# Two engines empty one PSUM result, a bank each, and the rounds of the second product are spread anew over a half block

## The chip, the cores and the metric

One core of one Trainium2 chip. The time is device time in microseconds (us) of one launch; a quoted time is the median of several executions. All executions of this study were of the same (fast) state, but those of one kernel still scatter by 2 to 4 us; the section on the start tells where much of that comes from. Where a few us matter I use the ratio of the mean times in the same rounds on the same chip, with its 95% interval.

## The reference

A causal convolution of 7 taps over time (softmaxed weights, one set per head of 24 channels), then a two-layer network with ELU, on 32768 tokens of 192 channels:

```python
# attention part: out[b,s,h,:] = sum_k softmax(weight)[h,k] * x_padded[b, s+k, h, :]
h = x @ w_in                                   # 192 -> 2048
g = np.where(h > 0.0, h, np.exp(np.minimum(h, 0.0)) - 1.0)
return (g @ w_out).astype(np.float32)          # 2048 -> 192
```

## The kernel before

The tokens go in 32 blocks of 1024; a block has 16 **pairs**, one for each 128 of the 2048 hidden channels. A pair is two products of 512 tokens, in one of three two-bank PSUM buffers H. ScalarE takes exp of it, GpSimd clamps it to at most 1, VectorE takes the maximum with h (I call its two instructions the pair's **clips**) and so frees the buffer. In the cuts, `W(s, n)` waits until semaphore `s` has counted to `n`:

```python
    # ScalarE, pair n
    W(s_h, n + 1)
    W(s_tt, 2 * (n - NE) + 2)
    for u in range(2):
        a.activation(E[:, n % NE, u, :], H[:, k, GS * u : GS * (u + 1)], ACT.Exp).then_inc(s_exp)
    # VectorE, pair n
    for n in range(NP):
        ...
        for u in range(2):
            W(s_clp, 2 * n + u + 1)
            v.scalar_tensor_tensor(out=gT[:, s % NG3, q, u, :], in0=E[:, n % NE, u, :], scalar=1.0,
                in1=H[:, slot_of_pair[n] % 3, GS * u : GS * (u + 1)],
                op0=ALU.subtract, op1=ALU.max).then_inc(s_tt)
```

The second product adds up in the last two banks, `ops`. It comes in **rounds** of two matmuls of 64x192, 64 rounds to a **half** of a block (256 + 256 tokens), placed in the gaps behind the pairs by a list of sizes. One conv (the convolution over time, for a later block) also stands in each half and takes a turn of the H buffers. When a half is done, ScalarE copies both banks at once:

```python
LAG = -3
GAPS = ((10,), (10,), (6,), (6,), (10,), (5, 6), (11,))     # rounds behind each pair of a half
EARLY_CONV = {3: (1, 0), 6: (1, 1), 9: (2, 0)}              # the first three convs, by pair
X_LATE = (17, 3, 2)                                         # an extra load of x, ahead of pair 17's clamp
...
    # ScalarE, end of a half
    W(s_swap, mm2_done[key])
    ...
    a.activation(osb[:, b, :, :, :].rearrange("p g k d -> p g (k d)"),
                 ops[:, :, 0 : 2 * D], ACT.Copy).then_inc(s_oev)
    # TensorE, first round of the next half
    W(s_oev, place[key])
```

## Time and profile before

| | before |
|---|---|
| time | 747.96 us (747.39 to 748.05, 3 executions) |
| steady block of 16 pairs | 22.54 us (27 blocks) |
| pair 10 / pair 16 begin | 28.2 / 35.9 us |
| VectorE / ScalarE / GpSimd busy | 85 / 87 / 89% |

A "steady block" is the time from the start of a pair to the start of the 16th pair after it, the mean from block 3 to block 29.

### The profile page before, as it was taken

The numbers are of one execution on the slowest core, as the hardware profiler recorded it, in microseconds if no ns is written. First come the engines' busy times: TensorE is split into PE (matmuls) and PEld (weight loads), VectorE is DVE, ScalarE is ACT, GpSimd is POOL, SyncE is SP. The second block draws the span as 40 slices with busy tenths as digits, with TensorE's granted clock in tenths as the row PEclk, the third lists the DMA queues.
The fourth block names the chain that finished last, engine by engine and source line by source line (L and its number), as shares of the span: only waits on it lengthen the run. The fifth ranks groups of instructions, "written<-read, shape, count | busy, mean of one in ns | idle before, by whom it ended". The sixth has DMA issues, their size and how long they took to land.

```text
span 746.5 us, 28038 instructions
## 1 busy us (share of the span) xinstructions
PE 731.6 (98%) x11866; PEld 505.4 (68%) x11866; DVE 638.0 (85%) x1042; ACT 646.8 (87%) x1224; POOL 664.5 (89%) x1108
## 2 busy tenths in 40 slices
PE   6899999999999999999999999999999999999997
PEld 3466667666766676666766766766766766766666
DVE  5789889889889888898898898898898898888894
ACT  4888988988988988888989989989989989889883
POOL 8799999999899999899999899999999899898893
PEclk9999999999999999999999999999999999999999
DMA  9544435535435535345535345635345444244212
GB/s 168 93 76 91 62 70 93 94 61 92 63 68 94 93 60 95 57 74 95 82 71 94 46 84 94 77 77 70 64 91 94 67 87 81 53 89 81 46 44 66
DMA packets 132881, 58.93 MB, mean 79 GB/s; under 512 B 98068, under 2 KB 132372, under 8 KB 132756
## 3 DMA queue, kind: packets, MB, share of 16 engines
q0 software_dynamic: 44160, 17.28, 22.9%
q1 hardware_dynamic: 88308, 39.37, 21.9%
q8 instruction: 93, 1.52, 0.9%
q10 hardware_dynamic: 288, 0.49, 0.2%
q14 instruction: 32, 0.26, 0.1%
HBM read 35.61 MB, written 25.17 MB: 81 GB/s over the span
## 4 chain that ended last, share of the span: by engine, by line
PE 93%; DVE 2%; POOL 2%; DMA 1%; ACT 1%; issue 0%
PE H L735 45%; PE ops L770 44%; PE H L703 3%; DVE gT L579 2%; DMA xg<-in_x_dram 1%; ACT E L515 1%; POOL E L414 1%; PE H L770 1%; POOL w_in L369 1%; ACT csb L485 0%; POOL xg L364 0%; PE ops L703 0%; ACT osb L474 0%; PE ops L615 0%; POOL sel L384 0%
## 5 line engine op out<-in xcount | busy, mean ns | idle before, releaser
L579 DVE SCALAR_TENSOR_TENSOR gT<-E,H 128x512 f16<-128x512 f32 x1024 | 632.5, 681 | 90.9 <-POOL E L414 84.4
L414 POOL TENSOR_SCALAR E<-E 128x512 f32<-128x512 f32 x1024 | 603.9, 615 | 69.5 <-ACT E L515 62.1
L515 ACT ACTIVATE E<-H 128x512 f32<-128x512 f32 x1024 | 546.2, 608 | 73.5 <-PE H L735 64.8
L770 PE MATMUL ops<-w_out,gT 64*128 64x192 f16 x8064 | 426.4, 243 | 0.3
L770 PEld LDWEIGHTS ops<-w_out,gT 64*128 64x128 f16 x8064 | 346.9, 94 | 110.5 <-ACT osb L474 11.4
L735 PE MATMUL H<-att,w_in 64*128 64x512 bf16 x3072 | 409.2, 378 | 2.9 <-DVE gT L579 1.7
L735 PEld LDWEIGHTS H<-att,w_in 64*128 64x128 bf16 x3072 | 130.9, 94 | 111.7 <-DVE gT L579 12.8
L485 ACT ACTIVATE csb<-H 128x480 bf16<-128x480 f32 x118 | 60.9, 568 | 7.4 <-PE H L703 0.4
L474 ACT ACTIVATE osb<-ops 128x768 f32<-128x768 f32 x63 | 52.0, 826 | 6.2 <-PE ops L770 6.2
L364 POOL DMA_DIRECT2D xg<-in_x_dram x62 | 55.7, 899 | 0.1
L703 PE MATMUL H<-xg,Tm 64*128 64x240 bf16 x472 | 44.0, 263 | 0.1
L703 PEld LDWEIGHTS H<-xg,Tm 64*128 64x128 bf16 x472 | 21.2, 94 | 0.8 <-DVE gT L579 0.3
L485 ACT ACTIVATE csb<-ops 128x480 bf16<-128x480 f32 x6 | 3.5, 588 | 3.2 <-PE ops L703 3.2
L770 PE MATMUL H<-w_out,gT 64*128 64x192 f16 x128 | 5.9, 243 | 0.0
L703 PE MATMUL ops<-xg,Tm 64*128 64x240 bf16 x24 | 2.7, 306 | 3.3 <-DMA xg<-in_x_dram 3.1
L590 DVE COPY osb<-H 128x192 f32<-128x192 f32 x1 | 0.4, 358 | 6.3 <-PE H L770 6.3
L770 PEld LDWEIGHTS H<-w_out,gT 64*128 64x128 f16 x128 | 5.3, 94 | 0.0
L369 POOL DMA_DIRECT2D w_in<-in_moe_w_in_dram x7 | 4.6, 663 | 0.3 <-DMA wh<-in_weight_dram 0.3
L610 PE MATMUL ops<-zw 128*128 128x512 bf16 x9 | 3.6, 577 | 1.2 <-DVE zw L527 1.2
L615 PE MATMUL ops<-zw 64*128 64x512 bf16 x12 | 2.4, 381 | 2.3 <-ACT csb L485 2.3
L703 PEld LDWEIGHTS ops<-xg,Tm 64*128 64x128 bf16 x24 | 0.9, 97 | 5.2 <-issue 3.5
L615 PEld LDWEIGHTS ops<-zw 64*128 64x128 bf16 x12 | 0.6, 93 | 4.2 <-ACT csb L485 3.9
(49 smaller groups left out, 26.3 us busy)
## 6 DMA issues: line engine op xcount, KB each, us to landing
out_dram<-osb SPq DMA_DIRECT2D x126, 192.0 KB, 4.1
xg<-in_x_dram POOLq DMA_DIRECT2D x61, 240.0 KB, 5.6
w_out<-in_moe_w_out_dram POOLq DMA_DIRECT2D x1, 768.0 KB, 16.1
att<-csb SPq DMA_TRANSPOSE x31, 6.4
w_in<-in_moe_w_in_dram POOLq DMA_DIRECT2D x2, 240.0 KB, 9.0
xf<-in_x_dram ACTq DMA_DIRECT2D x1, 384.0 KB, 3.2
xf<-in_x_dram SPq DMA_DIRECT2D x1, 384.0 KB, 3.6
w_in<-in_moe_w_in_dram POOLq DMA_DIRECT2D x2, 144.0 KB, 4.2
```

The source lines that it names most:

```text
L364: g.dma_start(xg[:, b, v0 : v0 + whole, :], src).then_inc(s_x[b][part - 1], 16)
L369: g.dma_start(w_in[HP * r : HP * (r + 1), :, c0:c1], moe_w_in.rearrange("(p j) f -> p j f", j=3)[:, :, c0:c1],).then_inc(s_w[k], 16)
L414: g.tensor_scalar(out=E[:, n % NE, u, :], in0=E[:, n % NE, u, :], scalar1=1.0, scalar2=0.0, op0=ALU.min, op1=ALU.max,).then_inc(s_clp)
L474: a.activation(osb[:, b, :, :, :].rearrange("p g k d -> p g (k d)"), ops[:, :, 0 : 2 * D], ACT.Copy,).then_inc(s_oev)
L485: return a.activation(csb[:, s % 2, :].rearrange("p (j v h i) -> p h j v i", j=3, v=2 * WPG, h=HEADS)[:, h0 : h0 + HB], conv_bank(m)[:, b, ...
L515: a.activation(E[:, n % NE, u, :], H[:, k, GS * u : GS * (u + 1)], ACT.Exp).then_inc(s_exp)
L579: v.scalar_tensor_tensor(out=gT[:, s % NG3, q, u, :], in0=E[:, n % NE, u, :], scalar=1.0, in1=H[:, slot_of_pair[n] % 3, GS * u : GS * (u + ...
L610: pe.matmul(ops[:, 0, :], zw[:, 0:P], zw[:], start=True, stop=True)
L615: pe.matmul(ops[:, r, :], zw[HP * r : HP * (r + 1), 0:P], zw[HP * r : HP * (r + 1), :], start=True, stop=True, tile_position=(HP * r, 0),)
L703: ins = pe.matmul(to[:, b, n1 * hh : n1 * (hh + 1)], Tm[HP * rt : HP * (rt + 1), h, :], xg[HP * rt : HP * (rt + 1), s % NXB, :, :].rearran ...
L735: ins = pe.matmul(H[:, k % 3, GS * r : GS * (r + 1)], w_in[HP * r : HP * (r + 1), j, FC * q : FC * (q + 1)], att[HP * r : HP * (r + 1), s ...
L770: ins = pe.matmul(acc[:, g, d0 : d0 + D], gT[HP * rt : HP * (rt + 1), t % NG3, q, g, t0 : t0 + P], w_out[HP * rt : HP * (rt + 1), q, :], s ...
```

## The change

Its intent: the two banks leave on two engines at once, so the evacuation is over sooner and ScalarE is relieved; the rounds are spread so that two light gaps follow the evacuation; and the first convs stand later, so that they don't wait for x.

```diff
-LAG = -3
-GAPS = ((10,), (10,), (6,), (6,), (10,), (5, 6), (11,))
+LAG = -5
+GAPS = ((), (1,), (16,), (7,), (7,), (7,), (6,), (7, 3, 10))
-EARLY_CONV = {3: (1, 0), 6: (1, 1), 9: (2, 0)}
+EARLY_CONV = {6: (1, 0), 8: (1, 1), 10: (2, 0)}
...
+            load_x(2, 2)
             g.dma_start(w_out ...)
-            load_x(2, 2)
...
-                a.activation(osb[:, b, ...], ops[:, :, 0 : 2 * D], ACT.Copy).then_inc(s_oev)
+                out_ready(W, key)
+                a.activation(*out_pieces(key, 0), ACT.Copy).then_inc(s_oev)
...  # VectorE
-            for n in range(NP):
+            for item in order:
+                if item[0] == "o":
+                    for key in item[2]:
+                        out_ready(W, key)
+                        v.tensor_copy(*out_pieces(key, 1)).then_inc(s_od)
+                elif item[0] == "h":
                     ...
...  # TensorE
                                 W(s_oev, place[key])
+                                W(s_od, place[key])
```

The end of the half now lies in the conv's own gap: 7 rounds, half a conv, 3 rounds, the other half, 10 rounds. VectorE's copy stands, in its program, behind the clips of that pair.

More of the change, by code (lines that the diff above doesn't have):

```diff
@@ L24 @@
 BN = HB * CPH * 2 * WPG
-GAP_SPLIT = 4
 TAP = 6
@@ L84, in bass_lightweight_conv__then__act_elu_kernel, with conv_at @@
     order = []
-    def conv_at(s, g, gap=None):
+    def conv_at(s, g, between=None):
         m = 2 * s + g - 2
@@ L90, in conv_at @@
         order.append(("c", m, 0))
-        between = []
-        if gap:
-            between, gap[:] = gap[:GAP_SPLIT], gap[GAP_SPLIT:]
         if between:
@@ L139, in bass_lightweight_conv__then__act_elu_kernel @@
         gaps = list(rounds_at.get(n, ()))
-        if len(gaps) == 2:
-            order.append(("o", gaps.pop(0)))
-        if n in EARLY_CONV:
-            conv_at(*EARLY_CONV[n])
-        if s:
-            for at, ahead, g in CONV_AT:
-                if at == i and s + ahead < NS:
-                    conv_at(s + ahead, g, gaps[0] if gaps else None)
-        if gaps and gaps[0]:
-            order.append(("o", gaps[0]))
+        convs = [EARLY_CONV[n]] if n in EARLY_CONV else []
+        convs += [
+            (s + ahead, g)
+            for at, ahead, g in CONV_AT
+            if at == i and s + ahead < NS and 2 * (s + ahead) + g - 2 >= FREE_CONV
+        ]
+        if convs and len(gaps) == 3:
+            order.append(("o", gaps[0]))
+            conv_at(*convs[0], gaps[1])
+            order.append(("o", gaps[2]))
+            continue
+        for conv in convs:
+            conv_at(*conv)
+        for gap in gaps:
+            order.append(("o", gap))
     last_slot = [take_slot(None) for _ in range(2)]
@@ L326, in out_group, with out_ready, out_pieces @@
             eng.dma_start(dst, osb[:, b, g, :, :]).then_inc(s_out[b], 16)
+        def out_ready(W, key):
+            t, half, kb = key
+            n_half = 2 * t + half
+            W(s_swap, mm2_done[key])
+            W(s_out[n_half % 2], 32 * (n_half // 2))
+        def out_pieces(key, g):
+            t, half, kb = key
+            b = (2 * t + half) % 2
+            if (t, half) == (last, 1):
+                return osb[:, b, g, kb, :], H[:, last_slot[kb] % 3, GS * g : GS * g + D]
+            return (
+                osb[:, b, g, :, :].rearrange("p k d -> p (k d)"),
+                ops[:, g, 0 : 2 * D],
+            )
         def turn_att(eng, s):
@@ L454, in evac @@
             def evac(key):
-                t, half, kb = key
-                n_half = 2 * t + half
-                W(s_swap, mm2_done[key])
-                b = n_half % 2
-                W(s_out[b], 32 * (n_half // 2))
-                if (t, half) == (last, 1):
-                    if kb == 0:
-                        a.activation(
-                            osb[:, b, :, 0, :],
-                            H[:, last_slot[0] % 3, :].rearrange("p (g t) -> p g t", g=2)[:, :, 0:D],
-                            ACT.Copy,
-                        ).then_inc(s_oev)
-                    else:
-                        a.activation(
-                            osb[:, b, 0, 1, :], H[:, last_slot[1] % 3, 0:D], ACT.Copy
-                        ).then_inc(s_oev)
-                        W(s_od, 1)
-                        out_group(a, t, half, 1, 1)
-                    return
-                a.activation(
-                    osb[:, b, :, :, :].rearrange("p g k d -> p g (k d)"),
-                    ops[:, :, 0 : 2 * D],
-                    ACT.Copy,
-                ).then_inc(s_oev)
+                out_ready(W, key)
+                a.activation(*out_pieces(key, 0), ACT.Copy).then_inc(s_oev)
+                if key == (last, 1, 1):
+                    W(s_od, place[key] + 1)
+                    out_group(a, last, 1, 1, 1)
             late = []
@@ L572, in _vector @@
             v.tensor_copy(Tm[:], Tr[:, :, ::-1]).then_inc(s_tm)
-            for n in range(NP):
-                s, q = divmod(n, NQ)
-                if s >= NG3:
-                    W(s_swap, mm2_done[s - NG3, 1, 0])
-                for u in range(2):
-                    W(s_clp, 2 * n + u + 1)
-                    v.scalar_tensor_tensor(
-                        out=gT[:, s % NG3, q, u, :],
-                        in0=E[:, n % NE, u, :],
-                        scalar=1.0,
-                        in1=H[:, slot_of_pair[n] % 3, GS * u : GS * (u + 1)],
-                        op0=ALU.subtract,
-                        op1=ALU.max,
-                    ).then_inc(s_tt)
-            b = (2 * NS - 1) % 2
-            W(s_swap, mm2_done[last, 1, 1])
-            W(s_out[b], 32 * (NS - 1))
-            v.tensor_copy(
-                osb[:, b, 1, 1, :], H[:, last_slot[1] % 3, GS : GS + D]
-            ).then_inc(s_od)
+            for item in order:
[4 more added lines that the diff above has]
+                elif item[0] == "h":
+                    n = item[1]
+                    s, q = divmod(n, NQ)
+                    if s >= NG3:
+                        W(s_swap, mm2_done[s - NG3, 1, 0])
+                    for u in range(2):
+                        W(s_clp, 2 * n + u + 1)
+                        v.scalar_tensor_tensor(
+                            out=gT[:, s % NG3, q, u, :],
+                            in0=E[:, n % NE, u, :],
+                            scalar=1.0,
+                            in1=H[:, slot_of_pair[n] % 3, GS * u : GS * (u + 1)],
+                            op0=ALU.subtract,
+                            op1=ALU.max,
+                        ).then_inc(s_tt)
         @block.tensor
@@ L814, in _sync @@
                         t, half, kb = key
-                        W(s_oev, place[key] + 1)
-                        if (t, half) != (last, 1):
-                            for g in range(2):
+                        for g in range(2):
+                            W((s_oev, s_od)[g], place[key] + 1)
+                            if (t, half) != (last, 1):
                                 out_group(sy, t, half, g)
-                        elif kb == 0:
-                            for g in range(2):
-                                out_group(sy, t, half, g, 0)
-                        else:
-                            out_group(sy, t, half, 0, 1)
+                            elif (g, kb) != (1, 1):
+                                out_group(sy, t, half, g, kb)
             for b in range(2):
```

## The prediction

> **What bounds the kernel now.** I read the page first, then the list of waits, then windows over single stretches, then the timeline of TensorE over one half block. The page gives TensorE 98% of the span, and the chain that ended last is almost all TensorE:
>
> ```profile
> PE 731.6 (98%) x11866; PEld 505.4 (68%) x11866; DVE 638.0 (85%) x1042; ACT 646.8 (87%) x1224; POOL 664.5 (89%) x1108
> ...
> L579 DVE SCALAR_TENSOR_TENSOR gT<-E,H 128x512 f16<-128x512 f32 x1024 | 632.5, 681 | 90.9 <-POOL E L414 84.4
> L414 POOL TENSOR_SCALAR E<-E 128x512 f32<-128x512 f32 x1024 | 603.9, 615 | 69.5 <-ACT E L515 62.1
> L515 ACT ACTIVATE E<-H 128x512 f32<-128x512 f32 x1024 | 546.2, 608 | 73.5 <-PE H L735 64.8
> ...
> L474 ACT ACTIVATE osb<-ops 128x768 f32<-128x768 f32 x63 | 52.0, 826 | 6.2 <-PE ops L770 6.2
> ```
>
> The reader should see three helpers at 85 to 89% behind a nearly full TensorE. Each of the 512 pairs (two 512-wide products into one of three H buffers) passes through ScalarE (exp), GpSimd (clamp) and VectorE (max), and only VectorE's second instruction frees the buffer. The finished output is read by ScalarE once a half, 63 times 826 ns.
>
> "98%" overstates how full TensorE is, because the span of a matmul includes its pipeline: six H matmuls show 0.82 us, but the next work starts 0.65 us after them. So I compare starts with starts. In the timeline of TensorE (start, duration):
>
> ```profile
> 308.13 0.83 PE L735 MATMUL H<-att,w_in 64*128 64x512 bf16 x6
> 308.78 1.01 PE L770 MATMUL ops<-w_out,gT 64*128 64x192 f16 x20
> 309.61 0.83 PE L735 MATMUL H<-att,w_in 64*128 64x512 bf16 x6
> 310.25 0.59 PE L770 MATMUL ops<-w_out,gT 64*128 64x192 f16 x10
> 310.96 0.38 PE L703 MATMUL H<-xg,Tm 64*128 64x240 bf16 x4
> ```
>
> A pair takes 0.65 us and a round (two matmuls side by side) 0.0825 us (0.83 for ten). Five rounds from 310.25 should end at 310.66, yet the conv starts at 310.96: 0.3 us of waiting for a buffer. From the starts of the pairs I took all steady periods: 22.50 or 22.57 us for a block of 16 pairs, so **11.26 us a half** (8 pairs, 64 rounds, one conv). The pure stream is 8 x 0.65 + 64 x 0.0825 + 0.46 for the two conv pieces = 10.94 us. So about 0.3 us a half is stalled, 62 halves x 0.3 = 19 us in all: that is the most that the steady part can give, 2.5% of 748.
>
> Who stalls it, from the list of waits (total us, times, longest):
>
> ```profile
> PEld H L735 <- DVE gT L579: 12.8, 42, 1.4
> PEld ops L770 <- ACT osb L474: 11.4, 62, 0.2
> ...
> PEld ops L615 <- ACT csb L485: 3.9, 3, 1.3
> ...
> PE ops L703 <- DMA xg<-in_x_dram: 3.1, 1, 3.1
> ```
>
> The first row is the H buffer, the second the evacuation. The second is a weight load's wait, 0.18 us each time, and TensorE itself lost none of it: after the 11 rounds come two pairs (1.30 us) without rounds, and the ten rounds after them start on time (313.72 to 315.02 is two pairs exactly). The evacuation is already hidden.
>
> **What the Trainium skill says.** "TensorE: Matmul & The Clock Gate", section "Back-to-back issue gap", gives N/2.4 + 2.5 ns between warm matmuls: 216 ns at 512 and 82.5 ns at 192. The trace agrees: 0.65 us for three side-by-side steps of 512, 0.083 for a round. "PSUM — Partial Sum Buffer", section "Specifications (TRN2)", says that ScalarE and VectorE can read PSUM in parallel at full bandwidth where they are on different banks; the trace has it once, in the very last copy: both started at 742.8 us on a bank each of one result, and took 331 (ScalarE) and 358 ns (VectorE), with no sign of one slowing the other. "VectorE: DVE Perf Modes", section "Why PSUM operands drop a tier", says that fp32 from PSUM runs at the 1x mode: that copy of 128x192 took 358 ns, and VectorE's casts out of PSUM of 256 and 512 columns 425 and 692, so 1.04 ns a column, and 384 columns should take 358 + 192 x 1.04 = 558 ns (estimate).
>
> **The change, part by part.**
>
> 1. Split evacuation. ScalarE: 826 becomes about 484 ns (the row of its 128x384 copy), 63 x 0.34 = 21 us less busy. VectorE: 63 x 0.56 = 35 us more, 638 to some 670 us (90%). The bank pair is free after about 0.6 us instead of 0.9. Since that wait cost TensorE nothing, the direct value is about zero. VectorE does its copy just after the clips of the conv step's pair, where it waits for GpSimd anyway: the next pair begins 2.8 us after that one, VectorE has a gap of about 1.6 us there, and 0.56 fits.
>
> 2. Spread of the rounds. What sets the stalls is how soon a buffer returns. Undisturbed, a pair's second clip ends 3.5 us after the pair begins (3.48 to 3.60 in the steady rows), and TensorE goes on 0.05 later: 3.55. Three buffers rotate, the conv taking a turn. So a pair must not come within 3.55 us of the third place before it, nor faster than VectorE's 1.20 us a pair for long. New half: conv step 0.65 + 7 x 0.0825 + 0.26 + 3 x 0.0825 + 0.25 + 10 x 0.0825 = 2.81; then 0.65 (no rounds), 0.73 (1), 1.97 (16), three of 1.23 (7), 1.15 (6): 11.0 us. Against the rule: the second pair after the conv step would begin 2.81 + 0.65 = 3.46 after the pair whose buffer it takes, a stall of 0.09; the fourth 0.65 + 0.09 + 0.73 + 1.97 = 3.44 after its own, a stall of 0.11; all others are 3.6 or later. Sum 11.2. The same walk over the old half, with VectorE's and GpSimd's queues in it, gives 11.22 where 11.26 is measured, so it is right to about 0.05. **Steady gain 0.02 to 0.06 us a half, near 2 us in 60 halves.** The pile-up moves from the pairs after the long empty stretch to the conv step; it does not go.
>
> 3. Start. Before, the first conv stands behind pair 3 and waits 3.1 us for x, after which the clock is halved:
>
> ```profile
> 18.00:21.40 3.40, 3.00 (x18) 1.17 (x20) 0.00 (x0) 1.09 (x3) 0.00 (x0) 0.51 1.59 193
> ```
>
> (the 0.51 is PEclk.) With the convs behind pairs 6, 8, 10 pairs 4 to 6 run in that time, paced by VectorE. But pair 10 needs the last part of w_in, which is copied within SBUF; that copy is issued at 20.1 us with 6.3 us to landing, so 26.4, and before pair 10 began at 28.2. New: pair 10 at 26.4, its conv, pairs 11 and 12, the first round held to about 30.3 by the conv's second evacuation, pair 13 at 30.4, pair 16 at about 34.9 against 35.9 before, with 5 rounds more done (0.4 us). **Gain 1.5 us**, not the 3 + 2.3 us of the removed waits.
>
> 4. Block 1. It took 23.3 us instead of 22.5, because a load issued on GpSimd (0.9 us) stood before pair 17's clamp and pair 19 waited for that buffer. The two start 0.65 + 6 x 0.0825 + 2.81 = 3.96 us apart in the new order and about 3.5 in the old, so some 0.3 to 0.4 us less is lost.
>
> 5. Tail. Both end in the same rounds and the same two single-bank copies; the last two halves without a conv may wait for the split evacuation, a few tenths. Zero net.
>
> Sum: 2 + 1.5 + 0.3 = 3.8 us; 748.0 - 3.8 = **744.2 us**.
>
> **Rivals.** (a) The stalls do go: the 3.5 us is a little shorter when queues are emptier, the two borderline gaps (3.46 and 3.44) fit, and a half takes 11.0: 60 x 0.25 = 15 us, plus the start, 731. For it: both misses are only about 0.1 us, and the split takes 0.34 us from ScalarE next to those pairs. Against: 3.48 is the minimum that I found, and ScalarE is not what frees the buffer. (b) VectorE becomes the bound: the 0.56 copy pushes the clips behind it, each half loses up to 0.3, some 760 us. For it: at 90% VectorE would be the busiest helper, and it takes its work in order, so a copy waiting for TensorE blocks clips. Against: the gap of 1.6 us. (c) The start gives nothing: an idle of about 3 us before pair 10 halves the clock in turn, as it did before, 746. For it: it is nearly as long as the old wait; against: the skill's first page above, section "What's actually happening", ties the halving to a window of about 3.4 us of idleness, and the idle may be split by window edges. The trace had 3.05 us idle and then 3.4 us at half clock.
>
> **Range and chances.** The steady part is 60 times a difference of -0.05 to +0.1 us, so -3 to +6 us; start and block 1 give 0 to 3. Range 738 to 749. Faster by over 2% (under 733) needs rival (a) almost whole: 0.07. Slower by over 2% (over 763) needs (b) at its worst: 0.03. Within 2%: 0.90.
>
> **What would show it.** Right: ScalarE rows 128x384 near 484 ns and VectorE COPY 128x384 near 560, TensorE's pair starts 11.2 us a half apart with the two small stalls behind the second and fourth pair after the conv step, no wait for xg at the first conv but a wait of some 3 us for w_in before pair 10, pair 16 at about 35. Wrong: halves of 11.0 (rival a) or over 11.3 with VectorE's copies as releaser of ops or H (rival b); a half-clock stretch near 27 us (rival c).

## The result, and the profile after

The change took 743.4 us (742.09 to 745.38, 4 executions); ratio 0.9943, interval 0.9915 to 0.9972. The kernel before took 747.87 us in the same rounds (4 executions). By the ratio the change is 4.3 us faster, and the predicted time was 744.2. A ratio is the mean time of one kernel's fast runs over that of the other's of the same rounds, so not quite the ratio of the medians.

The page of the changed kernel: busy time of each engine, the clip, and the two copies (line, engine, operation, shape, count; then busy us and mean ns of one; then idle time before it):

```profile
PE 730.0 (98%) x11866; PEld 501.9 (68%) x11866; DVE 657.9 (89%) x1106; ACT 636.3 (86%) x1224; POOL 663.9 (89%) x1108
...
L583 DVE SCALAR_TENSOR_TENSOR gT<-E,H 128x512 f16<-128x512 f32 x1024 | 622.1, 681 | 70.3 <-POOL E L431 69.9
...
L473 ACT ACTIVATE osb<-ops 128x384 f32<-128x384 f32 x63 | 31.3, 497 | 9.5 <-PE ops L769 9.5
L575 DVE COPY osb<-ops 128x384 f32<-128x384 f32 x63 | 34.6, 550 | 4.6 <-PE ops L769 4.6
```

ScalarE's copy is 497 ns (484 expected), VectorE's 550 (558 expected). But they do not run side by side, as was intended. The timelines of ScalarE and VectorE at one end of a half (start, duration):

```profile
311.49 0.50 ACT L473 ACTIVATE osb<-ops 128x384 f32<-128x384 f32 x1
311.87 0.55 DVE L575 COPY osb<-ops 128x384 f32<-128x384 f32 x1
```

VectorE is still at its clips when ScalarE begins, so the two overlap by 0.12 us (the median of the steady halves too), and the evacuation takes 0.93 us from end to end, longer than the 0.82 of the one copy before. What the change gains is not a sooner evacuation.

The timeline of TensorE around the end of a half (start, duration):

```profile
309.65 0.39 PE L701 MATMUL H<-xg,Tm 64*128 64x240 bf16 x4
309.90 0.42 PE L769 MATMUL ops<-w_out,gT 64*128 64x192 f16 x6
310.16 0.37 PE L701 MATMUL H<-xg,Tm 64*128 64x240 bf16 x4
310.42 1.00 PE L769 MATMUL ops<-w_out,gT 64*128 64x192 f16 x20
311.25 1.58 PE L733 MATMUL H<-att,w_in 64*128 64x512 bf16 x12
312.67 0.25 PE L769 MATMUL ops<-w_out,gT 64*128 64x192 f16 x2
```

Two pairs from 311.25 to 312.67 are 1.42 us where 1.30 is free running: a stall of 0.12. Such stalls are what is left in the steady part, and the list of waits shows who ends them:

```profile
PEld H L733 <- DVE gT L583: 30.8, 68, 1.3
...
PE H L733 <- DMA w_in<-w_in: 2.7, 1, 2.7
```

The ScalarE wait of the next half's first round is gone from the list; the wait for a clipped H buffer has grown (weight loads, 12.8 to 30.8 us). The list does not hold every stall, for all that a steady block takes 22.41 us instead of 22.54. The second row is the new wait at the start: pair 10 for w_in. Windows of the profiled run there (length, then busy us of each engine, granted clock, DMA share, GB/s):

```profile
21.40:24.70 3.30, 1.42 (x16) 0.52 (x14) 2.84 (x5) 3.22 (x8) 2.54 (x5) 1.00 1.38 206
24.70:28.10 3.40, 1.86 (x10) 0.58 (x10) 1.28 (x2) 0.78 (x2) 0.66 (x2) 0.50 0.88 167
28.10:31.50 3.40, 3.14 (x16) 1.03 (x16) 1.45 (x3) 2.69 (x7) 2.00 (x4) 0.50 0.04 8
```

The clock is at half speed for 6.8 us, so pair 16 begins at 36.2 us, later than before (35.9). This profiled run was the slowest of the four (745.4 us); two of the four, at 742.1, had a granted clock of 1.000 over the whole run.

### The profile page after: what moved, and what is told of

Read it like the earlier page. It is cut to its first block, busy times and chain, and to the rows that moved or that the text cites. A ratio compares the mean times of both kernels' runs of the same rounds, so it can differ in the third digit from the quotient of the medians.

```text
span 743.3 us, 28196 instructions
## 1 busy us (share of the span) xinstructions
PE 730.0 (98%) x11866; PEld 501.9 (68%) x11866; DVE 657.9 (89%) x1106; ACT 636.3 (86%) x1224; POOL 663.9 (89%) x1108
## 3 DMA queue, kind: packets, MB, share of 16 engines
q1 hardware_dynamic: 88308, 39.37, 20.7%
## 4 chain that ended last, share of the span: by engine, by line
PE 95%; DMA 3%; POOL 1%; DVE 0%; ACT 0%; issue 0%
PE ops L769 45%; PE H L733 45%; PE H L701 3%; DMA w_in<-in_moe_w_in_dram 2%; DMA w_in<-w_in 1%; PE H L769 1%; POOL E L431 1%; POOL w_in L386 1%; POOL xg L381 0%; DVE gT L583 0%; DMA wh<-in_weight_dram 0%; ACT E L513 0%; PE ops L701 0%; ACT csb L483 0%; DVE osb L575 0%
## 5 line engine op out<-in xcount | busy, mean ns | idle before, releaser
L583 DVE SCALAR_TENSOR_TENSOR gT<-E,H 128x512 f16<-128x512 f32 x1024 | 622.1, 681 | 70.3 <-POOL E L431 69.9
L733 PEld LDWEIGHTS H<-att,w_in 64*128 64x128 bf16 x3072 | 131.9, 94 | 108.2 <-DVE gT L583 30.8
L473 ACT ACTIVATE osb<-ops 128x384 f32<-128x384 f32 x63 | 31.3, 497 | 9.5 <-PE ops L769 9.5
L575 DVE COPY osb<-ops 128x384 f32<-128x384 f32 x63 | 34.6, 550 | 4.6 <-PE ops L769 4.6
L701 PEld LDWEIGHTS H<-xg,Tm 64*128 64x128 bf16 x472 | 18.3, 93 | 3.5 <-issue 1.2
```

The source lines that it names most:

```text
L473: a.activation(*out_pieces(key, 0), ACT.Copy).then_inc(s_oev)
L575: v.tensor_copy(*out_pieces(key, 1)).then_inc(s_od)
L701: ins = pe.matmul(to[:, b, n1 * hh : n1 * (hh + 1)], Tm[HP * rt : HP * (rt + 1), h, :], xg[HP * rt : HP * (rt + 1), s % NXB, :, :].rearran ...
L733: ins = pe.matmul(H[:, k % 3, GS * r : GS * (r + 1)], w_in[HP * r : HP * (r + 1), j, FC * q : FC * (q + 1)], att[HP * r : HP * (r + 1), s ...
```

## The experiments

Twelve kernels ran, all correct. Each quoted ratio is against the kernel before. Theories: that the split evacuation is hidden and worth nothing by itself (my prediction), against it shortening the queue of ScalarE; that the new order is what gains; that VectorE is or is not at its limit; and what the start is worth.

### 1. The new order with one engine's copy

```diff
-                a.activation(*out_pieces(key, 0), ACT.Copy).then_inc(s_oev)
+                a.activation(osb[:, b, ...], ops[:, :, 0 : 2 * D], ACT.Copy).then_inc(s_oev)   # both banks, but for the last half
```
and no copy on VectorE.

> The new order of rounds, but ScalarE copies both banks again (one 128x768 instruction, 0.82 us), VectorE none; only the last half stays split. Theory A (my prediction: the evacuation is hidden, so the split by itself is worth nothing): 743 us, halves of 11.2 us as with the change. Rival B (in the new order two pairs follow the evacuation at 0.75 us spacing, and ScalarE, 0.34 us longer in its copy, begins their exps later, which frees the H buffers later): my walk with the measured durations gives 11.30 a half, 0.1 more, so 62 x 0.1 = 6 us slower, some 749 us, with the stall at the pairs two and four after the conv step.

Measured: 751.04 us (749.73 to 752.19, 9 executions), ratio 1.0032 (1.0021 to 1.0043). The steady block is 22.61 us against 22.41 with the split. The page's row of the copy, and the wait for the H buffer:

```profile
L474 ACT ACTIVATE osb<-ops 128x768 f32<-128x768 f32 x63 | 51.5, 818 | 9.5 <-PE ops L777 9.5
```

```profile
PEld H L742 <- DVE gT L592: 44.1, 125, 1.4
```

So rival B holds: without the split the H buffer is waited for 125 times instead of 68, and the new order is, by itself, slower than the old kernel by 0.3%. The whole gain of the change, and more, is the split's: 751.0 to 743.7 (a second set of runs of the change, below) is 7 us, 6 us of it in the steady blocks and 1 us after pair 496 (35.0 us to the end against 34.0).

### 2. The old order with the split, twice

Everything of the old order, first convs and loads included, with the change's evacuation. First as the change has it, VectorE's copy behind the clips of the pair in whose gap the half ends:

> The old order of rounds, load order and first convs, but the evacuation split over ScalarE and VectorE. Theory A (the split is hidden and independent of the order): as before, 748 us. Rival B (VectorE takes its work in order, and in the old order a half ends right after the pair that it still has to clip; its copy comes after that pair's clips, 3.5 + 0.56 us after the pair began, while TensorE is back for the next half's first round 2.9 us after it): a stall of about 1.2 us a half at the ops bank, released by VectorE's copy, so 62 x 1.0 to 1.2 = 62 to 74 us slower, 810 to 822 us.

Measured: 814.38 us, ratio 1.0876 (1.0860 to 1.0893). Its waits, and VectorE's timeline at one end of a half:

```profile
PE ops L768 <- DVE osb L574: 67.0, 62, 1.5
```

```profile
302.21 1.28 DVE L582 SCALAR_TENSOR_TENSOR gT<-E,H 128x512 f16<-128x512 f32 x2 [0.89 <-POOL E L430]
303.41 0.55 DVE L574 COPY osb<-ops 128x384 f32<-128x384 f32 x1
303.88 2.47 DVE L582 SCALAR_TENSOR_TENSOR gT<-E,H 128x512 f16<-128x512 f32 x4
```

VectorE sat idle for 0.89 us, waiting for GpSimd, then clipped the pair, and only then copied, 62 times 1.08 us of TensorE's time, as rival B has it. "PSUM — Partial Sum Buffer", section "Engine vs sequencer instructions", says that the queues of ScalarE, VectorE and GpSimd are strictly first in, first out; this trace agrees. The second kernel lets the copy go first (but for the last pair, on whose clips the copy itself waits):

```diff
+            ahead, queue = [], []
             for item in order:
-                if item[0] == "o": ...       # copy
-                elif item[0] == "h": ...     # clips
+                if item[0] == "h":
+                    ahead = [item]
+                    queue.append(ahead)
+                elif item[0] == "o" and item[2]:
+                    ahead.insert(0 if ahead[-1][1] < NP - 1 else len(ahead), item)   # ahead of its pair's clips
+            for item in [item for step in queue for item in step]:
+                ...                          # copy or clips, as before
```

> The old order with the split evacuation as in the run that took 814 us, but VectorE's copy stands ahead of the clips of the pair of its step, not behind them. Theory A (the 66 us of that run are VectorE's program order: the copy sat behind clips that finish 3.5 us after the pair began): they go wholly, no wait of TensorE for VectorE's copy, halves of 11.2 to 11.3, some 745 to 749 us. Rival B (two engines' copies of one result, or VectorE's load as such, slow the old order): it stays above 770 us.

Measured: **737.99 us** (736.95 to 738.54), ratio 0.9868 (0.9855 to 0.9880): faster than both kernels. Theory A holds as to the 66 us, but the time lies 7 us under its range: that the split gains this much by itself was expected by neither. A steady block takes 22.20 us. VectorE and ScalarE of that run at one end of a half:

```profile
309.96 0.56 DVE L582 COPY osb<-ops 128x384 f32<-128x384 f32 x1 [0.44 <-PE ops L776]
310.44 1.27 DVE L590 SCALAR_TENSOR_TENSOR gT<-E,H 128x512 f16<-128x512 f32 x2
```

```profile
310.00 0.51 ACT L472 ACTIVATE osb<-ops 128x384 f32<-128x384 f32 x1
310.58 2.72 ACT L512 ACTIVATE E<-H 128x512 f32<-128x512 f32 x5
```

and ScalarE in the kernel before, at the same place of the order:

```profile
313.99 0.82 ACT L474 ACTIVATE osb<-ops 128x768 f32<-128x768 f32 x1
314.68 1.60 ACT L515 ACTIVATE E<-H 128x512 f32<-128x512 f32 x3
```

With the split and the copy first, the two copies do run side by side (309.96 and 310.00), and the banks are free after 0.56 us. In the kernel before, the pair after the copy begins at 313.72 and its exp at 314.68, 0.96 us later, the copy having held ScalarE; where nothing is in the way it is 0.86. In pair-by-pair records of one block (pairs 164 and 165, counted from pair 160) the exps begin 0.96 and 1.27 us after their pairs before, and 0.85 and 1.17 with the copy split and first. The clips of pairs 164 to 167 ended at 9.95, 11.14, 12.34 and 13.53 us before and at 9.75, 10.95, 12.14 and 13.34 now, and pairs 167, 168 and 169, which take those buffers, began 0.13 to 0.20 us earlier. The means over all steady blocks say the same: the clips of the two pairs after the copy end 3.59 and 4.14 us after their pairs begin before, 3.46 and 4.01 with the copy split and first. That is where the gain comes from: not the wait for the evacuated bank, but the exps queued behind the copy, and through GpSimd and VectorE the return of the H buffers.

### 3. Is VectorE at its limit?

```diff
                         v.tensor_copy(*out_pieces(key, 1)).then_inc(s_od)
+                        W(s_pad, place[key])
+                        v.tensor_tensor(xf[:, 1, 0:2, :], xf[:, 1, 2:4, :], xf[:, 1, 2:4, :], ALU.add).then_inc(s_pad)
```

> The change with one more VectorE instruction of 128x384 fp32 (an add within SBUF, some 0.4 to 0.5 us) right after each of VectorE's copies, which nobody waits for. Theory A (VectorE has a gap of 1.6 us there): within 1 us of the change, 743. Rival B (VectorE at 89% busy is the bound, every nanosecond there counts): 63 x 0.45 = 28 us slower, 771 us.

Measured: 743.65 us, ratio 0.9932 (0.9917 to 0.9947), the same as the change; steady block 22.40 us.

```profile
PE 728.3 (98%) x11866; PEld 501.0 (68%) x11866; DVE 687.7 (93%) x1171; ACT 636.0 (86%) x1224; POOL 662.3 (89%) x1108
...
L578 DVE TENSOR_TENSOR xf<-xf 128x384 f32<-128x384 f32 x65 | 35.7, 549 | 0.0
```

Theory A holds: thirty-six us more of work on VectorE, at 93% busy, cost nothing. (Its mean of 549 ns is over 65 records, two of them of the last half.) At that place it has room; experiment 2 showed the same 0.55 us costing 66 us at another. The busy share tells neither.

### 4. One round moved

```diff
-GAPS = ((), (1,), (16,), (7,), (7,), (7,), (6,), (7, 3, 10))
+GAPS = ((), (1,), (17,), (6,), (7,), (7,), (6,), (7, 2, 11))
```

> The change with 0,1,17,6,7,7,6 and 7+2+11 in place of 0,1,16,7,7,7,6 and 7+3+10: one round is moved ahead of the fourth pair after the conv step, which stalls by about 0.1 us for its H buffer, from the step behind it. Theory A (the stall is the buffer rule of 3.55 us): that stall goes, 0.03 us a half comes back, 2 us less than the change, 741. Rival B (the stall is moved to the next pair): same as the change within 1 us.

Measured: 743.68 us, ratio 0.9933 (0.9918 to 0.9948); steady block 22.40 us, as with the change. The gap behind which the round was put grew from 2.03 to 2.05 us only, so the stall in front of the fourth pair did go, but other gaps grew in its place (the conv's to 2.85 in one half, the last to 1.28). Rival B: the stall moved to the next pairs.

### 5. The start: four kernels

Only the first convs (and the order of two loads) moved, in the old order:

```diff
-EARLY_CONV = {3: (1, 0), 6: (1, 1), 9: (2, 0)}
+EARLY_CONV = {6: (1, 0), 8: (1, 1), 10: (2, 0)}
```

> The kernel before with only the first convs moved to steps 6, 8, 10 and the order of the last two early loads as in the change. Theory A (the start is worth what the change's start shows: pair 10 at 24.5 to 26.1 us instead of 28.1, and with a halved clock 1.3 us of it lost): 0 to 3 us less than before, 745 to 748, in two groups by the granted clock. Rival B (it only pays with the new order, since before the first round comes at step 13): same as before within 0.5 us.

Measured: 746.86 us (745.50 to 748.16, 21 executions), ratio 0.9986 (0.9980 to 0.9993): 1.0 us faster, so theory A. The granted clock sorts its executions, with little overlap: 745.50 to 746.50 us for the 7 at 1.000, 746.04 to 748.16 for the 14 below it. The other way round, the change with the old first convs and loads:

> The change with the first convs at steps 3, 6, 9 and the order of the last two early loads as before. Theory A (my prediction's start part, 1.5 us): 3.1 us of waiting for x come back at the first conv, with a halved clock from 18 to 21 us, but pair 10 no longer waits for w_in; 1 to 2 us slower than the change's fast group, 743.5 to 744. Rival B (the new place of the convs only exchanges one wait and one halved clock for another): equal to the change's slow group, 744.7 to 745.4, or better than it.

Measured: 744.99 us (744.44 to 745.51), ratio 0.9961 (0.9948 to 0.9973). By the ratios (0.9943 and, on the same chip and rounds, 0.9936 for the change) that is 1.3 to 1.9 us slower, what theory A has. Its times lie where rival B put them, but in the same rounds every execution of the change was faster (741.99 to 744.10), so B does not hold. The halved clock that theory A also named did not come in the profiled execution, where TensorE waited only 1.61 us for x. The new start is worth 1 to 2 us.

The changed kernel itself again:

> The changed kernel as it is, once more, for how often its clock is halved at the start. The first four executions were 742.1, 742.1 (granted clock 1.000), 744.7 (0.998) and 745.4 us (0.995). Theory: the idle of some 3 us before pair 10 halves the clock in some executions only[...]; two groups of times, near 742 and near 745, go with a granted clock of 1.000 and below it.

Measured: 743.69 us (741.99 to 744.10, 5 executions), ratio 0.9936 (0.9922 to 0.9950). The two groups did not show cleanly: 741.99 and 743.19 had a clock of 1.000, 743.69 to 744.10 0.998 or 0.999. Dummy work in the wait for w_in:

```diff
+                    if n == 10:                      # into pair 10's own H buffer, ahead of its wait for w_in
+                        for _ in range(12):
+                            for r in range(2):
+                                pe.matmul(H[:, k % 3, GS * r : GS * (r + 1)], zw[...], zw[...], start=True, stop=True, ...)
+                        W(s_wc, 16)
```

> The change with 12 pairs of dummy matmuls (2.6 us) into pair 10's own H buffer while it waits for w_in, so that TensorE is not idle there. Theory A (the halved clock at the start is caused by that idle time and costs the 3 us between the two groups): all executions near 742 us at a granted clock of 1.000, no slow group. Rival B (the slow group has another cause, say DMA): the spread of 742 to 745 stays.

Measured: 743.51 us (743.28 to 743.90, 5 executions), ratio 0.9941 (0.9929 to 0.9954). All five had a clock of 1.000, where two of five had it without the dummy work in the same rounds, and the scatter fell to 0.6 us: so the halved clock there comes from that idle time, as theory A says. But there were no runs at 742 either: in this run's trace w_in had landed at 24.3 us, and the 2.75 us of dummy work kept pair 10 back to 25.9. The padding costs what it saves.

With what the traces tell, most of the scatter of the start can be put in two rules. In the traces with these early convs the copy of w_in within the core's memory lands anywhere from 24.3 to 26.1 us. Where pair 10 waits for it, pair 16 begins 8.5 us after pair 10 at full clock (24.54 to 33.04, and 25.94 to 34.42), and 9.7 to 10.0 after it when the clock is halved (25.49 to 35.23, 26.15 to 36.20). So pair 16 began anywhere from 33.0 to 36.2 us with the same early convs, and the spans of these runs follow: 740.0 for 33.0, 742.1 for 35.2, 743.3 for 36.2. The rules leave out a third cause: in nine of the fourteen profiled executions pair 0 begins at 10.7 to 11.0 us, in the other five at 12.3 to 13.3, for the matmuls ahead of it run slower there. This goes with no one kernel's edit, and I did not test it.

### 6. The start: mending it

The second half of w_in's last part straight from DRAM:

```diff
-            load_w_in(3, (0,))
+            load_w_in(3, (0, 1))
...
-            W(s_w[3], 16)
-            sy.dma_start(w_in[HP:P, :, c0:c1], w_in[0:HP, :, c0:c1]).then_inc(s_wc, 16)
```

> The change with the second half of the last part of w_in loaded from DRAM right behind the first, in place of the copy within SBUF that is issued only when the first has landed (19.9 us) and lands at 26.1. Theory A (pair 10 waits for that copy alone): it lands near 21 to 22 us, pair 10 begins near 24 us and not at 26.2, the idle time and the halved clock go, 2 to 2.5 us less than the change's fast group: 739.5 to 740. Rival B (the DMA queues are full at that time, and the 288 KB push the loads behind it, x for the third conv and w_out, later by as much): the wait moves to the third conv or to the first round, same as the change.

Measured: 742.74 us (741.53 to 743.73), ratio 0.9928 (0.9914 to 0.9942), not separable from the change. In the trace w_in landed at 20.7 us and pair 10 began at 23.5, as theory A said, yet pair 16 began at 33.07, as in the best run with the copy. The wait had moved on, to the places that rival B names:

```profile
25.35 0.83 PE L701 MATMUL ops<-xg,Tm 64*128 64x240 bf16 x8 [1.09 <-ACT csb L483]
```

the third conv, right behind pair 10, waits 1.09 us for the evacuation of the second conv, whose last part ScalarE takes only after another pair's exps, and the first round behind waits as long for the third's. It is ScalarE that is waited for, and not the loads that rival B blames. So w_in matters only where it lands after some 24.5 us.

The extra load of x, with the change:

```diff
-X_LATE = (17, 3, 2)
+X_LATE = (10, 3, 2)
```

> The change with the extra load of x, issued on GpSimd ahead of pair 17's clamp, issued ahead of pair 10's instead, where GpSimd is idle. Theory A (block 1 is long because that 0.9 us issue delays pair 17's clamp and with it pair 19's H buffer): the block from pair 16 to pair 32 takes 22.5 us instead of 23.2, 0.7 us less in all, 743.0 against 743.7. Rival B (that load then competes with w_in and w_out at the start): pair 10 or the first round begins later by as much.

Measured: 743.22 us (741.87 to 744.84), ratio 0.9943 (0.9929 to 0.9956). The block from pair 16 to 32 took 22.39 us instead of 23.17, as theory A said; the 0.8 us is not to be seen in the times, which scatter by 3.

All three together, with the first convs at 5, 7 and 9:

> All that the runs point to for the start: the change with the last part of w_in loaded directly, the extra load of x issued ahead of pair 10's clamp, and the first convs at steps 5, 7, 9, so that each conv's evacuation, which held the third conv and the first round by 1.1 us each in the run with direct w_in, is done earlier. Theory A: pair 16 begins near 32 us instead of 33.1 (w_out lands at 27.3 and then holds the first round), block 1 takes 22.5, 742.7 - 1.1 - 0.7 = 741 us, no halved clock. Rival B (the pairs are paced by the clips at 1.2 us at the start anyway): pair 16 at 33, 742 us.

Measured: 741.79 us (741.04 to 742.15, 4 executions), ratio 0.9919 (0.9906 to 0.9932), no halved clock before the end, block 1 at 22.38 us. Its pair 0 began late (12.29 us): not because of x, which landed at 5.29 us against 5.21 in the best run with the change's own start (experiment 3), but because the matmuls between ran slower (one group of 22 took 1.47 us, 0.88 in the profiled run of the change). Pair 16 began 22.1 us after pair 0, against 22.0 in the best run with the change's own start: the pairs are paced by the clips there, as rival B says, and moving the convs gained nothing. The times scatter by 1.1 us only, and by the ratios they are some 0.2% better than the change's, but the intervals overlap. It was not run together with the old order and the copy that goes first, so what the two give together is open.

## Why the prediction was right, point by point

**The sum was right, several of its terms were not.** 744.2 was said, 743.4 measured, but the parts (of one profiled execution each, where no ratio is meant):

| step | said | measured |
|---|---|---|
| steady half, by the walk | 11.2 us | 11.2 us (22.41 a block) |
| steady part | near 2 us faster | 3.4 us faster, from pair 32 to pair 496 |
| evacuation of both banks | 0.6 us instead of 0.9 | 0.93 us instead of 0.82 |
| split alone | "about zero" | 7 us in the new order, 10 in the old |
| order of the rounds alone | 2 us faster | 0.3% slower, steady block 22.61 for 22.54, in spite of a better start |
| start | 1.5 us | 1.0 us in the old order, 1.3 to 1.9 in the new |
| block 1 | 0.3 to 0.4 us | 23.17 for 23.33, 0.2 us; over a steady block it is 0.76 for 0.79, so nothing but the steady gain |
| tail | 0 | from pair 496 to the end 34.0 us in both |
| busy time | ScalarE 21 us less, VectorE 35 more | 10.5 less, 19.9 more |

So that the sum fell within 1 us of the result is in part luck: the steady part gave more than was said, and the start less in some executions and more in others.

**The walk was right about the new order, and had the new gaps in it.** It put the two remaining stalls at the second and the fourth pair after the conv step, and the starts show them: that step is 2.83 us (2.81 said), then 0.76, 0.74, 2.03, 1.24, 1.23, 1.22, 1.14 (0.74, 0.73, 2.08, three of 1.23, 1.15 said). Here too there is some luck. As the prediction shows it, the walk gave every pair 3.55 us until its buffer is back, and so it left ScalarE's copy out. The clips of the two pairs after the copy end 3.91 and 4.36 us after their pairs begin (means of the steady blocks), but in the new order those two buffers are asked for only 4.0 and 4.5 us after, so it did not show. In the kernel before, the same numbers were 3.59 and 4.14. With ScalarE's long copy put in, the same walk gave 11.30 us for a half of experiment 1, and 22.61 a block was measured.

**The step that failed is the attribution.** The sentence "Since that wait cost TensorE nothing, the direct value is about zero" looked only at who waits for the copied bank. The copy also stands in ScalarE's queue ahead of the exps of two pairs, so a copy that is 0.33 us shorter brought the H buffers of these pairs back about 0.1 us sooner (3.59 to 3.46 and 4.14 to 4.01 in experiment 2), and that was the bound. Likewise rival (a) did not come true (halves of 11.2 us and not 11.0), but it was dismissed with "ScalarE is not what frees the buffer": it does not free it, but it begins the chain that does. "The pile-up moves ... it does not go" was right about the new order, but understated: by itself, the new order makes things slightly worse. What it does is make room for VectorE's copy behind the clips.

**Rival (b)** was rightly put low for the change: no wait of TensorE for VectorE's copy is left there, and experiment 3 gave VectorE another 36 us for nothing. But the danger named with it, a copy that stands in order among the clips, is real: 66 us in the old order.

**The start.** The wait for x went, and pair 10 waited for w_in until 26.15 us where 26.4 was said. The halved clock of rival (c) came in some executions and not in others; in the profiled one it ate the whole gain (pair 16 at 36.2 instead of 34.9), in the traces at full clock pair 10 came sooner than I had said (24.5 us in the best).

## What to carry to other kernels

An instruction off the critical path costs what stands behind it in its engine's queue: before calling a wait hidden, look at what the same engine does next, not only at who waits for the result. When work moves to another engine, its place in that engine's program decides: here the same 0.55 us copy cost 66 us behind two clips and gained 10 us ahead of them, without any new schedule of the rounds. And test the parts of a joint change alone; here one part carried all of the gain and the other took some back.

## What the Trainium skill lacked or had wrong

- "TensorE: Matmul & The Clock Gate", section "What's actually happening", gives about 3.4 us of idleness for the halved clock. Here shorter idle times came before it: 1.97, 1.98 and 2.20 us in three runs (then one stretch of 3.4 us at half clock), 2.71 us in another (then 6.8 us, with TensorE busy in 55% of the first stretch and 92% of the second). Waits of 0.97, 1.10, 1.58 and 1.61 us in that stage of four other runs had no halved clock behind them. The longest wait alone does not decide it, though: in two runs a half-clock stretch began at 7.7 and 8.4 us with no longer wait between matmuls before it than 0.97 and 1.29 us. Whether it came varied between executions of one kernel.
- "PSUM — Partial Sum Buffer", section "Specifications (TRN2)", says that ScalarE and VectorE read different banks side by side at full bandwidth: nearly so here. The same two copies took 513 and 557 ns where they ran at once (experiment 2, copy first) and 498 and 551 where they ran apart (copy behind the clips), so 3% and 1% longer.
- No page that I read says what the place of an instruction in a helper's program is worth; the page above says only that the queues keep their order. Here: 814.4 against 738.0 us for the same instructions, VectorE's copy behind or ahead of two clips.
